# Linear attention into a Swish MLP on one Trainium2 core: a block of small matmuls moved into the output product, and two VectorE differences grouped with a norm multiply

## The chip, the core and the metric

The kernel runs on one core of one Trainium2 chip. The metric is the device time of one execution in microseconds (us): the median of three runs. All other times here are from one profiled execution, counted from the start of its span, whose length is a little under the device time.

The core has five engines, each with its own queue of instructions that it takes in order: TensorE (PE; weight loads are listed apart as PEld), VectorE (DVE), ScalarE (ACT), GpSimd (POOL) and SyncE (SP, which here only issues transfers). They wait for each other through semaphores. TensorE writes only to PSUM, of which there are eight banks (PS0 to PS7 in the kernel).

## The reference, cut to what matters

```
q, k, v: [8 batches, 8 heads, 576, 64]
q_s = softmax(q) over the 64          # exp(q) / sum
k_s = softmax(k) over the 576
kv  = k_s^T v                         # 64 x 64 for each batch and head
x   = q_s kv, heads side by side      # [4608 tokens, 512]
h   = x w_in                          # [4608, 2048]
g   = h * sigmoid(beta * h)
out = g w_out                         # [4608, 512]
```

## The kernel before, in words

**Slabs.** The 4608 tokens are worked in nine slabs. Slab t, for t from 0 to 7, holds the first 512 tokens of batch t; slab 8 holds the remaining 64 tokens of all eight batches. A slab has two passes. Pass 1 makes h and g: 16 tiles of 128 columns of w_in, each from four matmuls (L406) of 128 x 512, then a SiLU on ScalarE (L744) and a scaling by 1/beta on VectorE (L767). Pass 2 makes the output product.

**Pass 2 with seven products.** From slab 1 on, `pass2_fast` uses a scheme of the Strassen kind: in place of eight block products there are seven, each of 16 matmuls of 128 x 256 (L844). The first uses sums of blocks of g (`GS1`), the next two `GS2`, both written during pass 1 (L798, L803); the last two use differences of blocks of g, which `g_diff(0)` and `g_diff(1)` (L810) write in place into GT on VectorE. The combination of the results is on VectorE (TS: L915, L918, L924, L892) and ScalarE (L880). The three accumulators are called s, z5 and z2; z2 is bank OB[1].

**The attention of later batches.** In the same slabs the attention of the next batches is prepared. ScalarE makes exp(q) and exp(k) (L319; for the 64 remaining tokens L331 and L346). `norm_main` makes the softmax of q: VectorE sums (L357) and takes the reciprocal (L359), and the multiply by it (L361) is on GpSimd or on VectorE. `norm_turn` is `norm_main` for two pairs of heads with the multiply on GpSimd, followed by `turn`, a transfer by the DMA engines that transposes EQ into QT (L606). `cast_v` and `cast_vr` convert v on GpSimd (L377, L391). `kv_all` makes k_s^T v with 40 small matmuls (L482), which VectorE scales into KVD (L490, L459). Then `quad` multiplies KVD with QT in 64 x 64 tiles of the TensorE array (L554) and evacuates the results to XT, the input of the next slab's pass 1: blocks 0 and 2 on VectorE, 1 and 3 on ScalarE (L596). From slab 4 on, `quad` also handles the 64 remaining tokens of two batches, from QTR to XT8 (L579).

**What sets the order.** The order within each queue is the order in which the Python code adds instructions. Two devices interleave the work. A counter, `tick`, advances by 1 for each matmul of pass 1 (64 in a slab) and by 32/56 for each matmul of pass 2; a list `todo` names pieces of work with the slot at which they are added, such as slot 97. And `hooks` name work to be added at points of pass 2: `at(0)` ahead of the first product, `at(3)` behind the third, `at(4)` behind the fourth, and so on. So work with a slot over 64 falls into pass 2. Waits are derived from the keys that each instruction reads and writes, and from the PSUM banks that it touches. In `quad` the first matmul takes all the waits of the block: for KVD and QT, and for every bank that it will use, among them those of the last tiles of pass 1.

Three places matter here. In slabs 4 to 6, `quad` for the next batch is added at the head of `pass2_fast`, ahead of `at(0)`, with the line

```
if 3 < t < 7:
    quad(t + 1, (0, 1), t - 3)
```

In slabs 1 and 2, `at(3)` holds `norm_turn(b, 2)` for the second half of the heads, then `g_diff(0)`, then the load of a later batch. In the same slabs `kv_all` is at slot 97, `g_diff(1)` just behind it at 97.01, and the first half of `quad` at 118; its second half follows at slot 1.5 of the next slab. Slab 2 further has, at `at(4)`, exp(q) and the v casts of batch 4. Slab 3 does its `g_diff(1)` and its whole `quad` at slots 99 and 112; slabs 4 to 6 do both differences together behind the third product.

Of the kernel before, what the change touches and what calls it, by code (L numbers as in the profile page):

```python
# [158 lines left out]
def bass_efficient_attn_shen__then__act_swish_beta_kernel(  # L159
# [12 lines left out]
    with ExitStack() as es:  # L172
# [176 lines left out]
        def norm_main(b, hp0, n, eng=DVE, sums=True, mult=True):  # L349
            i = b % 2  # L350
            a = bass.AP(EQ[i], hp0 * 512, [[2048, 128], [64, 8 * n], [1, 64]])
            s_ = bass.AP(QS[i], hp0 * 8, [[32, 128], [1, 8 * n]])
            v_ = bass.AP(QI[i], hp0 * 8, [[32, 128], [1, 8 * n]])
            vb = bass.AP(QI[i], hp0 * 8, [[32, 128], [1, 8 * n], [0, 64]])
            ks = [("eq", i, hp) for hp in range(hp0, hp0 + n)]
            if sums:
                add(DVE, lambda e: e.tensor_reduce(s_, a, AX.X, ALU.add), r=ks,  # L357
                    w=[("qs", i, hp0)])
                add(DVE, lambda e: e.reciprocal(v_, s_), r=[("qs", i, hp0)], w=[("qi", i, hp0)])  # L359
            if mult:  # L360
                add(eng, lambda e: e.tensor_tensor(a, a, vb, ALU.mult), r=ks + [("qi", i, hp0)],  # L361
                    w=ks)
# [35 lines left out]
        def bank(pool=MB):  # L398
            rot[0] += 1
            return pool[rot[0] % len(pool)]  # L400
# [42 lines left out]
        def kd(b):  # L443
            return b if b < 2 else 2 + b % 4
# [89 lines left out]
        def quad(b, gs=(0, 1), pi=None):  # L534
            i = b % 2
            if len(gs) == 1:
                bks = [bank(), bank()]
            else:
                bks = list(MB) + [HB[(hrot[0] + 1) % 3], HB[(hrot[0] + 2) % 3], OB[1]]
            b_x = {2 * g + a: bks[2 * n + a] for n, g in enumerate(gs) for a in range(2)}  # L540
            b_r = bks[4:6]
            rem = pi is not None
            used = list(b_x.values()) + (b_r if rem else [])
            first = [dict(
                r=[k_ for g in gs for c in range(2)
                   for k_ in (("kvd", kd(b), 2 * g + c), ("qt", i, 2 * g + c))]
                + ([("kvd", kd(2 * pi + e_), hp) for e_ in range(2) for hp in range(NHP)]
                   + ["qtr"] if rem else []), bank=used)]

            def tile(o, l, r_, a, c, bk, keys):  # L550
                kw = dict(r=keys, bank=[bk])
                if first:
                    kw = first.pop()
                add(PE, lambda e: e.matmul(o, l, r_, start=True, stop=True,  # L554
                                           tile_position=(64 * a, 64 * c), skip_group_check=True),
                    w=[("ps", bk)], **kw)

            def x_mm(g, a):
                rows = slice(64 * a, 64 * a + 64)
                for c in range(2):  # L560
                    hp, bk = 2 * g + c, b_x[2 * g + a]
                    tile(PS[bk][64 * c:64 * c + 64, :], KVD[kd(b)][rows, hp, 0:D],
                         QT[i][rows, hp, :], a, c, bk, [("kvd", kd(b), hp), ("qt", i, hp)])

            def r_mm(a):
                rows, bk = slice(64 * a, 64 * a + 64), b_r[a]
                for g in range(2):
                    for e_ in range(2):
                        for c in range(2):
                            hp, d, o = 2 * g + c, kd(2 * pi + e_), 128 * g + 64 * e_  # L570
                            tile(PS[bk][64 * c:64 * c + 64, o:o + 64], KVD[d][rows, hp, 0:D],
                                 QTR[rows, hp, 64 * e_:64 * e_ + 64], a, c, bk,
                                 [("kvd", d, hp), "qtr"])

            def r_evac(a):
                bk = b_r[a]
                o = bass.AP(XT8, a * SM + pi * 128, [[NM * SM, 128], [2 * SM, 2], [1, 128]])
                p = bass.AP(PS[bk], 0, [[512, 128], [128, 2], [1, 128]])
                add(DVE, lambda e: e.tensor_copy(o, p), r=[("ps", bk)], w=[("xt8", pi, a)],  # L579
                    bank=[bk])  # L580

            if rem:
                r_mm(1)
                x_mm(0, 0)
                x_mm(0, 1)
                x_mm(1, 0)
                x_mm(1, 1)
                r_mm(0)
                r_evac(1)
            else:  # L590
                for g in gs:
                    for a in range(2):
                        x_mm(g, a)
            for x in sorted(b_x):
                eng, bk = (DVE, ACTE)[x % 2], b_x[x]
                add(eng, lambda e, eng=eng, x=x, bk=bk: (  # L596
                    e.copy if eng == ACTE else e.tensor_copy)(XT[i][:, x, :], PS[bk][:, :]),
                    r=[("ps", bk)], w=[("xt", i, x)], bank=[bk])
            if rem:
                r_evac(0)  # L600

        def turn(b, hp0, n):
            i = b % 2
            o = bass.AP(QT[i], hp0 * 512, [[2048, 128], [128, 4 * n], [1, 128]])
            a = bass.AP(EQ[i], hp0 * 512, [[2048, 128], [1, 512 * n]])
            add(SP, lambda e: e.dma_start_transpose(o, a),  # L606
                r=[("eq", i, hp) for hp in range(hp0, hp0 + n)],
                w=[("qt", i, hp) for hp in range(hp0, hp0 + n)], slot=f"tq{i}{hp0}")
# [14 lines left out]
        def one(fn, *a):  # L623
            return lambda: fn(*a)

        def steps(fn, *a):
            return lambda: go(fn(*a))
# [2 lines left out]
            return kv_steps(b, (0, 1)) + kv_steps(b, (2, 3))  # L630

        def attn(b):
            return [(24 if b == 5 else 16, steps(kv_all, b))]

        def attn_late(b):
            if b < 4:
                return [(97, steps(kv_all, b)), (97.01, lambda: g_diff(1)),
                        (118, one(quad, b, (0,)))]
            return [(96, steps(kv_all, b)), (99, lambda: g_diff(1)), (112, one(quad, b))]

        def spread(steps, lo, hi):
# [9 lines left out]
        def go(steps):  # L651
            for s in steps:
                s()
# [137 lines left out]
        def gv(f, th, n):  # L791
            return GT[:, f:f + n, 256 * th:256 * th + 256]
# [15 lines left out]
        def g_diff(fh):  # L808
            f, th = NG * fh, 1 - fh
            add(DVE, lambda e: e.tensor_tensor(gv(f, th, NG), gv(f, th, NG), gv(f, 1 - th, NG),  # L810
                                               ALU.subtract),
                r=gk(f, 0, NG) + gk(f, 1, NG), w=gk(f, th, NG), war=True)
# [20 lines left out]
        def pass2_fast(t, tick, hooks):  # L833
# [67 lines left out]
                for f in hooks.get(n, ()):  # L901
                    f()

            if 3 < t < 7:
                quad(t + 1, (0, 1), t - 3)
            at(0)
            def prod_s(part):
                prod(s, lambda i, u: GS1[:, i, 128 * u:128 * u + 128], lambda i: [("gs1", i)],
# [46 lines left out]
        for t in range(NSLAB):  # L955
# [88 lines left out]
            def on(n, fn, *a):  # L1044
                hooks.setdefault(n, []).append(lambda: fn(*a))

            def exps(b):
                exp_q(b)
                exp_k(b)
                if b % 2 == 0:  # L1050
                    exp_kr(b)

            def casts(b):
                g = P.writer[("gs2", NG - 1)]
                if b % 2 == 0:
                    cast_vr(b, after=g)
                for hp in range(NHP):
                    cast_v(b, hp, after=g)

            if t == 1:  # L1060
                on(0, exps, 2)
                on(0, casts, 2)
                on(2, norm_turn, 2, 0)
                on(3, norm_turn, 2, 2)
                on(3, g_diff, 0)
                on(3, load, 4)
            elif t == 2:
                on(0, exps, 3)
                on(2, norm_turn, 3, 0)
                on(3, norm_turn, 3, 2)  # L1070
                on(3, g_diff, 0)
                on(3, load, 5)
                on(4, exp_q, 4)
                on(4, casts, 4)
                on(6, norm_turn, 4, 0)
            elif t == 3:
                on(0, exp_k, 4)
                on(0, exp_kr, 4)
                on(0, exp_q, 5)
                on(3, g_diff, 0)  # L1080
                on(4, norm_turn, 5, 0)
                on(5, norm_turn, 5, 2)
                on(4, exp_qr, 1)
                on(5, exp_k, 5)
                on(5, norm_turn_rem)
                on(5, casts, 5)
                on(5, load, 6)
                on(7, load_rem, "qrf", qt_h, QRF, 4)
            elif t + 2 < B:
                b = t + 2  # L1090
                on(0, exps, b)
                on(0, casts, b)
                if t == 4:
                    on(0, load, 7)
                on(3, norm_turn, b, 0)
                on(4, norm_turn, b, 2)
# [40 lines left out]
```

The softmax here doesn't subtract the row's maximum and nothing guards it: scores larger than these inputs give would overflow.

## Time and profile before

| | |
|---|---|
| device time, median of 3 | 275.91 us (275.74 to 276.08) |
| profiled span | 273.8 us |
| TensorE clock granted | 1.00 |
| slab 1, pass 2 | 60.75 to 74.92 |
| slab 2, pass 2 | 89.20 to 103.22 |
| slab 3, pass 2 | 117.66 to 131.41 |
| slabs 4, 5 and 6, from about the end of pass 1 to the end of pass 2 | 146.1 to 160.17, 174.9 to 189.10, 203.6 to 217.85 |
| slab 7, pass 2 (nothing else on TensorE) | 231.90 to 244.13 |

Slab 7 shows what the seven products take alone: 12.23 us. What the other slabs take more is the small matmuls of the attention and the time in which TensorE waits. In the profile's lines, a group is named by the line of the kernel that added it, its engine, operation and operands, with the number of instructions after an x. In the time lines the first number is the start, the second the length, and what stands in brackets at the end is the idle time ahead and what ended it. In the waits the numbers are the total, how often, and the longest.

### The profile page before, as it was taken

To read this page: it belongs to the slowest core of one execution; us is meant where nothing else is said; L and a number is where in the kernel's file an instruction comes from. 1 tells how busy PE (TensorE), PEld (TensorE's weight loads), DVE (VectorE), ACT (ScalarE), POOL (GpSimd) and SP (SyncE) were. 2 spreads that over 40 slices of the span, in tenths; PEclk is the share of its full clock that TensorE was granted. 3 is DMA by queue.
4 is the path that set the end of the run, shared out by engine and by line. 5 is a ranking of instruction groups with operands and counts; after the bars stand their busy time and mean duration, and the time that the engine had idled before them with its cause. 6 is when DMAs were issued, how large, how long until landed. Compare 5 with 4: busy or idle time off the path is not lost.

```text
span 273.8 us, 5005 instructions
## 1 busy us (share of the span) xinstructions
PE 264.2 (97%) x1993; PEld 163.5 (60%) x1993; DVE 192.1 (70%) x407; ACT 181.0 (66%) x287; POOL 62.0 (23%) x80
## 2 busy tenths in 40 slices
PE   8999999999999999999998999899989999999994
PEld 2444444458744874487545864487438845874683
DVE  4964586887868799769778766867586549625762
ACT  4897568788287957797767847793874377008610
POOL 2790010007430099002800470127000100000000
PEclk9999999999999999999999999999999999999999
DMA  7999999989799039920599999203600130012006
GB/s 212 320 204 207 227 329 350 290 246 377 143 347 290 36 73 313 307 78 2 101 342 230 340 319 156 92 4 77 211 2 0 22 153 0 2 47 109 0 0 156
DMA packets 59367, 45.95 MB, mean 168 GB/s; under 512 B 28608, under 2 KB 58320, under 8 KB 58320
## 3 DMA queue, kind: packets, MB, share of 16 engines
q1 hardware_dynamic: 54480, 40.90, 53.4%
q0 software_dynamic: 4240, 4.19, 9.3%
q10 hardware_dynamic: 624, 0.53, 0.6%
q8 instruction: 16, 0.26, 0.4%
q14 instruction: 7, 0.06, 0.1%
HBM read 36.71 MB, written 9.44 MB: 169 GB/s over the span
## 4 chain that ended last, share of the span: by engine, by line
PE 82%; DVE 7%; DMA 4%; POOL 2%; SPq 2%; issue 1%; ACT 1%; POOLq 0%; DVEq 0%
PE PS L406 49%; PE PS L844 30%; DMA VF<-in_v_dram 2%; DVE QS L357 2%; PE PS L554 1%; DMA QT<-EQ 1%; ACT GT L744 1%; DVE GT L810 1%; PE PS L482 1%; POOL VB L377 1%; SPq L290 1%; SPq L278 1%; DVE EQ L361 1%; POOL EQ L361 1%; DVE VB L377 1%
## 5 line engine op out<-in xcount | busy, mean ns | idle before, releaser
L406 PE MATMUL PS<-XT,WIN 128*128 128x512 bf16 x576 | 127.9, 379 | 0.1
L744 ACT ACTIVATE GT<-PS,BETA 128x512 bf16<-128x512 f32 x144 | 95.0, 689 | 37.2 <-PE PS L406 36.9
L406 PEld LDWEIGHTS PS<-XT,WIN 128*128 128x128 bf16 x576 | 54.9, 98 | 65.0 <-DVE XT L596 0.8
L767 DVE TENSOR_SCALAR GT<-GT,RB 128x512 bf16<-128x512 bf16 x144 | 52.6, 386 | 38.9 <-ACT GT L744 38.1
L361 POOL TENSOR_TENSOR EQ<-EQ,QI 128x1024 bf16<-128x1024 bf16 (+1 forms) x13 | 25.6, 1967 | 50.3 <-DVE QI L359 49.6
L844 PE MATMUL PS<-WOUT,GS 128*128 128x256 bf16 x256 | 30.6, 273 | 0.0
L844 PE MATMUL PS<-WSUM,GT 128*128 128x256 bf16 x256 | 29.9, 273 | 0.3 <-DVE GT L810 0.3
L844 PE MATMUL PS<-WOUT,GT 128*128 128x256 bf16 x256 | 29.8, 273 | 0.0
L880 ACT COPY O2S<-PS 128x512 f32<-128x512 f32 (+1 forms) x17 | 9.4, 559 | 28.4 <-PE PS L844 28.3
L844 PEld LDWEIGHTS PS<-WSUM,GT 128*128 128x128 bf16 x256 | 24.8, 98 | 4.1 <-issue 1.3
L844 PEld LDWEIGHTS PS<-WOUT,GS 128*128 128x128 bf16 x256 | 25.1, 98 | 2.9
L844 PEld LDWEIGHTS PS<-WOUT,GT 128*128 128x128 bf16 x256 | 24.8, 98 | 3.0
L319 ACT ACTIVATE EQ<-QF 128x512 bf16<-128x512 f32 x32 | 17.9, 619 | 7.7 <-DMA QF<-in_q_dram 7.5
L803 DVE TENSOR_TENSOR GS<-GT 128x512 bf16<-128x512 bf16 (+2 forms) x32 | 21.9, 685 | 0.0
L810 DVE TENSOR_TENSOR GT<-GT 128x2048 bf16<-128x2048 bf16 x16 | 21.2, 1353 | 0.0
L357 DVE TENSOR_REDUCE QS<-EQ 128x16 f32<-128x1024 bf16 (+1 forms) x20 | 19.7, 984 | 0.8 <-ACT EQ L319 0.8
L377 POOL CAST VB<-VF 128x512 bf16<-128x512 f32 x24 | 14.7, 613 | 22.7 <-DVE GS L803 13.8
L319 ACT ACTIVATE EK<-KF 128x512 bf16<-128x512 f32 x32 | 18.1, 620 | 0.2 <-DMA KF<-in_k_dram 0.2
L892 DVE TENSOR_TENSOR O2S<-TS,PS 128x512 f32<-128x512 f32 (+1 forms) x17 | 10.7, 644 | 9.3 <-PE PS L844 9.3
L844 PE MATMUL PS<-WSUM,GS 128*128 128x256 bf16 x128 | 16.6, 273 | 0.0
L406 PE MATMUL PS<-WOUT,GT 128*128 128x512 bf16 x64 | 15.4, 379 | 0.0
L798 DVE TENSOR_TENSOR GS<-GT 128x256 bf16<-128x256 bf16 (+2 forms) x32 | 13.6, 426 | 1.1
(88 smaller groups left out, 206.8 us busy)
## 6 DMA issues: line engine op xcount, KB each, us to landing
out_dram<-O2S SPq DMA_DIRECT2D x8, 1024.0 KB, 5.0
QF<-in_q_dram SPq DMA_DIRECT2D x6, 1024.0 KB, 6.6
KF<-in_k_dram SPq DMA_DIRECT2D x6, 1024.0 KB, 9.3
VF<-in_v_dram SPq DMA_DIRECT2D x6, 1024.0 KB, 12.4
KF<-in_k_dram SPq DMA_DIRECT2D x8, 256.0 KB, 5.6
VF<-in_v_dram SPq DMA_DIRECT2D x8, 256.0 KB, 5.6
WOUT<-in_moe_w_out_dram POOLq DMA_DIRECT2D x4, 512.0 KB, 16.5
WIN<-in_moe_w_in_dram POOLq DMA_DIRECT2D x3, 512.0 KB, 9.2
```

The lines of the kernel that those rows point to most:

```text
L319: add(ACTE, lambda e, o=o, a=a: e.activation(o, a, ACT.Exp), r=[(name + "f", i, hp)], w=[("e" + name, i, hp)])
L357: add(DVE, lambda e: e.tensor_reduce(s_, a, AX.X, ALU.add), r=ks, w=[("qs", i, hp0)])
L361: add(eng, lambda e: e.tensor_tensor(a, a, vb, ALU.mult), r=ks + [("qi", i, hp0)], w=ks)
L377: add(eng, lambda e: (e.copy if eng == ACTE else e.tensor_copy)(o, a), r=[("vf", i, hp), ("vone", i)], w=[("vb", i, hp)], after=after)
L406: add(PE, lambda e: e.matmul(o, l, r_, start=start, stop=stop), r=r, w=w, bank=[bk])
L744: add(ACTE, lambda e: e.activation(GT[:, f, :], PS[bk][:, :], ACT.Silu, scale=BETA[:, f:f + 1]), r=[("ps", bk), "beta"], w=[("gt", f, 0), ...
L767: add(DVE, lambda e: e.tensor_scalar(GT[:, f, :], GT[:, f, :], RB[:, f:f + 1], None, ALU.mult), r=k + ["rb"], w=k)
L798: add(DVE, lambda e: e.tensor_tensor(GS1[:, i:i + n, :], gv(i, 0, n), gv(i + NG, 1, n), ALU.add), r=gk(i, 0, n) + gk(i + NG, 1, n), w=[("g ...
L803: add(DVE, lambda e: e.tensor_tensor(GS2[:, i:i + n, :], GT[:, i:i + n, :], GT[:, i + NG:i + NG + n, :], ALU.add), r=[k_ for f in (i, i + ...
L810: add(DVE, lambda e: e.tensor_tensor(gv(f, th, NG), gv(f, th, NG), gv(f, 1 - th, NG), ALU.subtract), r=gk(f, 0, NG) + gk(f, 1, NG), w=gk(f ...
L844: add(PE, lambda e, l=l, r_=r_, st=st, u=u, i=i, b_=b_: e.matmul(PS[b_][:, 256 * u:256 * u + 256], l, r_, start=st, stop=end and i == NG - ...
L892: add(DVE, lambda e, b_=b_, u0=u0, u1=u1: e.tensor_tensor(o[:, u0:u1, :], ts[:, u0:u1, :], bank3(b_)[:, u0:u1, :], ALU.add), r=["ts", ("ps ...
```

## The change

It has two parts. In slabs 4 to 6 the block of 64 x 64 matmuls is no longer added ahead of the output product but at slot 72 of the `todo` list, so eight slots, or 14 matmuls of pass 2, after pass 1 ends. Its purpose is to let TensorE start the product while the last tile of pass 1 is still being read from PSUM.

In slabs 1 and 2, both differences stand together at `at(3)`, and the second multiply of the norm is taken from GpSimd to VectorE and put behind them: sums and reciprocal, two differences, multiply, transposing transfer. `g_diff(1)` leaves slot 97.01, and slab 1's `kv_all` moves from slot 97 to 100. Its purpose is to keep GpSimd's multiply out of the way of the differences.

```diff
         def attn(b):
-            return [(24 if b == 5 else 16, steps(kv_all, b))]
+            return [(24 if b == 5 else 16, steps(kv_all, b)),
+                    (72, one(quad, b, (0, 1), b - 4))]
 
         def attn_late(b):
             if b < 4:
-                return [(97, steps(kv_all, b)), (97.01, lambda: g_diff(1)),
-                        (118, one(quad, b, (0,)))]
+                return [(100 if b == 2 else 97, steps(kv_all, b)), (118, one(quad, b, (0,)))]
...
-            if 3 < t < 7:
-                quad(t + 1, (0, 1), t - 3)
             at(0)
...
+            def diffs_norm(b):
+                norm_main(b, 2, 2, mult=False)
+                g_diff(0)
+                g_diff(1)
+                norm_main(b, 2, 2, sums=False)
+                turn(b, 2, 2)
+
...
-                on(3, norm_turn, 2, 2)
-                on(3, g_diff, 0)
+                on(3, diffs_norm, 2)
...
-                on(3, norm_turn, 3, 2)
-                on(3, g_diff, 0)
+                on(3, diffs_norm, 3)
```

## The prediction

> **What bounds the kernel now.** I read the page's busy shares first, then the chain of waits, then TensorE's waits, then the time lines of the slabs that the diff touches. All times are microseconds from the span's start.
>
> ```profile
> PE 264.2 (97%) x1993; PEld 163.5 (60%) x1993; DVE 192.1 (70%) x407; ACT 181.0 (66%) x287; POOL 62.0 (23%) x80
> ```
>
> TensorE is busy for 97%. Only what stops TensorE, or adds to its list, changes the time; the other engines count where TensorE waits for them. The chain that ended last shows the stops of slab 4, and the same at 175.05 and 203.81 for slabs 5 and 6:
>
> ```profile
> 137.51 8.75 PE PS L406 x40
> 146.29 0.70 ACT GT L744
> 146.98 0.25 issue
> 147.23 0.77 PE PS L554 x20
> 148.00 12.33 PE PS L844 x112
> ```
>
> Columns: start, length, what. The chain leaves TensorE for the SiLU of the last tile of pass 1 (ACT GT L744), crosses a 0.25 hand-over and comes back with the small matmuls of `quad` (L554). In TensorE's waits it is the largest entry:
>
> ```profile
> PE PS L554 <- ACT GT L744: 2.9, 3, 1.0
> ```
>
> Three waits, 2.9 together. The product (L844) behind them needs none of this. Slab 2, by engine: VectorE and GpSimd.
>
> ```profile
> 97.23 1.26 DVE L810 TENSOR_TENSOR GT<-GT 128x2048 bf16<-128x2048 bf16 x1
> 98.41 0.16 DVE L490 RECIPROCAL RC<-PS 128x2 f32<-128x2 f32 x1
> 98.60 0.29 DVE L459 TENSOR_TENSOR KVD<-PS,RC 128x128 bf16<-128x128 f32 x1
> 98.81 0.16 DVE L490 RECIPROCAL RC<-PS 128x2 f32<-128x2 f32 x1
> 99.00 0.29 DVE L459 TENSOR_TENSOR KVD<-PS,RC 128x128 bf16<-128x128 f32 x1
> 99.20 2.12 DVE L810 TENSOR_TENSOR GT<-GT 128x2048 bf16<-128x2048 bf16 x1
> ```
> ```profile
> 95.50 4.74 POOL L361 TENSOR_TENSOR EQ<-EQ,QI 128x1024 bf16<-128x1024 bf16 x2 [13.77 <-DVE QI L359]
> 100.38 2.16 POOL L391 CAST VR<-VRF 64x512 bf16<-64x512 f32 x2
> 102.67 2.64 POOL L377 CAST VB<-VF 128x512 bf16<-128x512 f32 x4
> ```
>
> The reader should see two differences of one size at 1.26 and 2.12, and two GpSimd multiplies at 4.74 where one alone takes 1.90: they took turns. And TensorE in slabs 1 and 2:
>
> ```profile
> 67.80 0.22 PE L482 MATMUL PS<-VR,EKR 128*64 128x65 bf16 x2 [0.30 <-ACT EKR L331]
> ...
> 72.71 0.41 PE L554 MATMUL PS<-QT,KVD 64*64 64x512 bf16 x4
> ```
> ```profile
> 100.58 0.41 PE L554 MATMUL PS<-QT,KVD 64*64 64x512 bf16 x4
> 100.92 0.28 PE L844 MATMUL PS<-WSUM,GT 128*128 128x256 bf16 x1
> 101.47 1.91 PE L844 MATMUL PS<-WSUM,GT 128*128 128x256 bf16 x16 [0.27 <-DVE GT L810]
> ```
>
> The 40 small matmuls of `kv_all` (L482) stop for exp(k) of the remainder in slab 1; in slab 2 the last product stops for the second difference. The last entry of each line is the idle time and what ended it. For prices, the groups by shape:
>
> ```profile
> L361 DVE TENSOR_TENSOR EQ<-EQ,QI 128x512 bf16<-128x512 bf16 x7 | 5.1, 723 | 0.2
> ```
>
> [...] the second multiply (start 97.48, 2.76) is longer by 0.86 beside the first difference, and the second difference by 0.86 beside that multiply. [...] The norm multiply has a float32 factor; its median at 512 elements is 691 ns[...]. [...] In slab 3, where `quad` already stands inside a product, its start came 0.19 after the last full matmul's start instead of the usual 0.11: 0.08 for the switch in.
>
> **Part 1: the quads of slabs 4 to 6 move from the head of pass 2 to slot 72.** Pass 1 has 64 slots, a matmul of pass 2 counts 32/56, so slot 72 is 14 matmuls in. The last pass-1 matmul of slab 4 starts at 145.87; at that pace (0.216) the next could start at 146.09, and `quad` starts at 147.23: a stop of 1.14. Afterwards the first 14 product matmuls go there. They need bank `s`, whose SiLU ended at 145.25, and sums GS1 0 to 5 and GS2 0, done before 146. They last 14 x 0.109 = 1.53, so `quad` comes at 147.6, after the SiLU has been seen (147.23): no wait. It adds the switch in, 0.08 to 0.12. Saved: 1.14 - 0.10 = 1.04 per slab, 3.1 for three.
>
> What moves with it: on ScalarE the casts of x=1 and x=3 fall behind the exponentials. From table load to exp(q) remainder that is 155.52 - 148.92 = 6.6; from 146.98 it ends at 153.6, the two casts (1.07) at 154.7, and the copy of z5 (0.58) at 155.2. TensorE wants that bank at 156.68 - 1.04 = 155.6: hidden, by 0.4 less hand-over. The next readers of XT come with the next slab. On VectorE the four evacuations last from 147.94 to 149.88 today; moved, they are released by 148.0 and end near 149.9, and the TS copy queued behind them wants to start at 151.20 - 1.04 = 150.16: hidden. So is the product that needs the bank OB[1], at 150.3.
>
> **Part 2, slab 1.** Removed: a GpSimd multiply (1.90), which overlaps, and the stop for exp(k) of the remainder, since `kv_all` starts 3 slots = 5 matmuls = 0.55 later (67.73, the operand is there at 67.74, wanted 0.15 into the block). `kv_all` took 1.24 (67.18 to 68.42) and 0.76 in slab 2: 0.48 saved there. Added on VectorE: from 68.78 two differences at 1.18 start to start (2.35 for two where nothing interferes), to 71.14, then the multiply, [...] next instruction after 1.14: 72.28. No GpSimd work is queued in this stretch. Behind it stand RC and KVD (0.49); TensorE waits for KVD with `quad` of heads 0,1: 72.28 + 0.49 + 0.15 hand-over = 72.92, against 72.71. It would have arrived near 72.1, so the 0.48 goes into this wait and 0.2 is lost. The transpose of the second half is issued at 72.36 instead of 71.82 and lands 3.1 later, at 75.5; the second `quad` half is wanted at 75.65: hidden. With 3.7, as the first transpose took, it would cost 0.4. Slab 1: +0.2.
>
> **Part 2, slab 2.** Here GpSimd is not idle: with its second multiply gone, the casts for batch 4 follow at once (ready, since they start without a wait today). The first VR cast is waiting when the first difference ends at 98.41, so I let the two engines alternate as in the lines above: cast (0.55, the end of the stretched one: 101.25 to 101.80), second difference, cast, multiply. 98.41 + 0.5 + 1.1 + 0.5 + 1.1 = 101.6, with slab 1's 0.2, 101.8; KVD and hand-over 0.64: `quad` at 102.4 against 100.58, +1.8. From there to the first pass-1 matmul that needs the third XT block, VectorE has the block, a sum, a reduction with reciprocal, a sum and the next block, 3.8 plus 0.6, against 4.55 today (100.58 to 105.13): -0.15. The second difference is no longer waited for, which is inside that 4.55. Slabs 1 and 2 together: **+1.65**. Nothing gives it back: TensorE runs pass 1 of slab 3 without gaps.
>
> Sum: 275.91 - 3.1 + 1.65 = **274.5**.
>
> **The rivals.** (a) [...] For it: they are queued back to back, and no GpSimd instruction in this trace waits at the seam of two such instructions, so that the seam's winner isn't shown. Against: at 134.49 and 135.09, between casts started at 133.74, 134.41 and 135.08, VectorE's scalings took 0.6 instead of 0.35: the engines alternate. Then the multiply ends at 97.23 + 2.36 + 1.14 + 0.2 = 100.9, `quad` starts at 101.6, slabs 1 and 2 cost 0.85: 273.7. (b) Half of part 1 is lost, to a dearer switch of array modes in mid-product or to ScalarE's later casts and copy: -1.5, and the slabs' +1.65: 276.1, no change. For it: the margin of 0.4 on ScalarE in slab 4. Against: slab 5 has no remainder of k (0.5 less on ScalarE) and slab 6 no exponentials but one; slab 3's `quad` in mid-product shows no such cost. (c) Slower: the same with the slow transpose (+0.4) and one more GpSimd cast of 0.6 ahead of the multiply: 277.1. Against it: the casts have to come in just at each gap.
>
> **How the numbers follow.** Alternation 0.58, (a) 0.26, (b) 0.09, (c) 0.07. Faster is the first two, 0.84. The range goes from (a) with 0.4 more (the switches free, 0.3, and slab 1 nearer to no loss, 0.1), 273.3, to the forecast with 1.0 more (transpose 0.4, one more cast 0.6), 275.5; beyond lie (b) and (c).
>
> **What would show it.** Right: no TensorE wait of L554 on ACT GT L744 and some 27.7 instead of 28.75 (slab 6: 189.10 to 217.85) per slab for 4 to 6; in slab 1 no wait on EKR but `quad` held by KVD; in slab 2 VectorE's second difference and multiply lengthened by about 0.5 beside VR casts, and `quad` near 102.4. Wrong: `quad` in slab 2 before 101.8 (then (a)), or a new wait of L844 on ACT O2S or DVE in slabs 4 to 6 (then (b)).

## The result, and the profile after

| | before | changed | ratio (95% interval) |
|---|---|---|---|
| device time, median of 6 | 275.89 us | 274.42 us (274.0 to 274.77) | 0.9947 (0.9934 to 0.996) |
| profiled span | 273.8 us | 272.4 us | |

The changed kernel is faster by 1.5 us, against a forecast of 1.4. The two parts work against each other: the first gives about three microseconds, the second takes more than half of them back.

TensorE's waits in the changed kernel (total, how often, longest):

```profile
PE PS L554 <- DVE RC L490: 1.5, 1, 1.5
...
PE PS L554 <- DVE KVD L459: 1.0, 1, 1.0
```

The entry of L554 on ACT GT L744, 2.9 us in three waits, is gone. In its place stand two waits of the same small matmuls, one in each of slabs 1 and 2. The profile puts both down to VectorE; in slab 1 the transposed QT landed later than KVD was written, as shown below. The chain that ended last, at the seam of slab 4:

```profile
139.35 8.58 PE PS L406 x39
147.93 1.64 PE PS L844 x15
149.57 0.70 PE PS L554 x20
150.27 10.69 PE PS L844 x97
```

The chain no longer leaves TensorE here: pass 1, 1.64 us of product, `quad`, the rest of the product. It is 15 matmuls of the product that go ahead, not the 14 named above: 14 steps of 32/56 add up in floating point to just under 8, so slot 72 is reached at the fifteenth. The first pass-1 matmuls of slabs 4 to 7 now start at 133.31, 161.02, 188.72 and 216.43: 27.7 us a slab. Before it was 131.41, 160.17, 188.93 and 217.69: 28.76 a slab. (The table ahead ends slabs 5 and 6 with the last product matmul, 0.17 later.)

Now slab 2, where the time is lost. VectorE, then GpSimd, then TensorE in time lines of the changed kernel:

```profile
97.57 2.80 DVE L810 TENSOR_TENSOR GT<-GT 128x2048 bf16<-128x2048 bf16 x2
100.29 1.63 DVE L361 TENSOR_TENSOR EQ<-EQ,QI 128x1024 bf16<-128x1024 bf16 x1
101.85 0.16 DVE L490 RECIPROCAL RC<-PS 128x2 f32<-128x2 f32 x1
102.04 0.29 DVE L459 TENSOR_TENSOR KVD<-PS,RC 128x128 bf16<-128x128 f32 x1
```
```profile
95.84 1.90 POOL L361 TENSOR_TENSOR EQ<-EQ,QI 128x1024 bf16<-128x1024 bf16 x1 [13.77 <-DVE QI L359]
97.88 2.97 POOL L391 CAST VR<-VRF 64x512 bf16<-64x512 f32 x2
```
```profile
99.13 1.80 PE L844 MATMUL PS<-WSUM,GT 128*128 128x256 bf16 x15
102.47 0.41 PE L554 MATMUL PS<-QT,KVD 64*64 64x512 bf16 x4 [1.55 <-DVE RC L490]
...
106.82 1.47 PE L406 MATMUL PS<-XT,WIN 128*128 128x512 bf16 x6 [0.23 <-DVE XT L596]
```

Two VR casts that take 1.35 us when alone (in the run with held casts, below) now take 2.97, and the VectorE instructions beside them are longer too. KVD, which used to be written at 98.6, is written at 102.04 and ends at 102.33; 0.14 later `quad` starts. The profile names RC L490 as the releaser, which is the second reciprocal, started at 102.25; by the keys `quad` waits for the KVD ahead of it.

Slab 1 has no GpSimd work at that place, and its lines are the undisturbed price:

```profile
68.72 2.39 DVE L810 TENSOR_TENSOR GT<-GT 128x2048 bf16<-128x2048 bf16 x2
71.04 1.21 DVE L361 TENSOR_TENSOR EQ<-EQ,QI 128x1024 bf16<-128x1024 bf16 x1
72.17 0.16 DVE L490 RECIPROCAL RC<-PS 128x2 f32<-128x2 f32 x1
72.36 0.29 DVE L459 TENSOR_TENSOR KVD<-PS,RC 128x128 bf16<-128x128 f32 x1
```

2.39 against 2.80 and 1.21 against 1.63: each of the two casts adds 0.41 to 0.42 us in slab 2.

What `quad` waits for in slab 1 is the later of two: the KVD that its first half reads ended at 72.65, but the transpose of the first half of the heads took 4.1 us to land, until 73.0. `quad` started just behind it:

```profile
L606 SPq DMA_TRANSPOSE QT<-EQ x1: 1347/1347/1347, 68.9 to 68.9; - x1
...
DMA to landing us min/median/max: 4.1/4.1/4.1
```
```profile
73.05 0.41 PE L554 MATMUL PS<-QT,KVD 64*64 64x512 bf16 x4 [0.97 <-DVE KVD L459]
```

### The profile page after: what moved, and what is told of

It reads as the page before. It is cut to its first block, busy times and chain, and to the rows that moved or that the text cites. A ratio compares the mean times of both kernels' runs of the same rounds, so it can differ in the third digit from the quotient of the medians.

```text
span 272.4 us, 4985 instructions
## 1 busy us (share of the span) xinstructions
PE 262.3 (96%) x1974; PEld 163.5 (60%) x1993; DVE 193.9 (71%) x409; ACT 180.8 (66%) x287; POOL 58.8 (22%) x78
## 4 chain that ended last, share of the span: by engine, by line
PE 81%; DVE 12%; DMA 2%; SPq 2%; issue 1%; ACT 0%; DVEq 0%
PE PS L406 48%; PE PS L844 30%; DVE QS L357 3%; DMA VF<-in_v_dram 2%; DVE GT L810 2%; DVE EQ L361 2%; PE PS L554 1%; PE PS L482 1%; SPq L278 1%; SPq L290 1%; DVE QI L359 1%; DVE O2S L892 1%; DVE VB L377 1%; DVE TS L913 1%; DVE TS L916 1%
## 5 line engine op out<-in xcount | busy, mean ns | idle before, releaser
L406 PE MATMUL PS<-XT,WIN 128*128 128x512 bf16 x560 | 125.4, 379 | 1.5 <-issue 0.3
L744 ACT ACTIVATE GT<-PS,BETA 128x512 bf16<-128x512 f32 x144 | 95.0, 689 | 37.4 <-PE PS L406 37.2
L844 PE MATMUL PS<-WOUT,GS 128*128 128x256 bf16 x256 | 31.1, 273 | 0.0
L361 POOL TENSOR_TENSOR EQ<-EQ,QI 128x1024 bf16<-128x1024 bf16 (+1 forms) x11 | 20.0, 1822 | 50.5 <-DVE QI L359 50.2
L844 PE MATMUL PS<-WOUT,GT 128*128 128x256 bf16 x256 | 29.8, 273 | 0.0
L844 PE MATMUL PS<-WSUM,GT 128*128 128x256 bf16 x256 | 29.8, 273 | 0.0
L880 ACT COPY O2S<-PS 128x512 f32<-128x512 f32 (+1 forms) x17 | 9.4, 560 | 27.6 <-PE PS L844 27.6
L844 PEld LDWEIGHTS PS<-WSUM,GT 128*128 128x128 bf16 x256 | 24.8, 98 | 3.7 <-issue 0.9
L844 PEld LDWEIGHTS PS<-WOUT,GT 128*128 128x128 bf16 x256 | 24.8, 98 | 2.9
L844 PEld LDWEIGHTS PS<-WOUT,GS 128*128 128x128 bf16 x256 | 24.8, 98 | 3.0
L377 POOL CAST VB<-VF 128x512 bf16<-128x512 f32 x24 | 16.4, 682 | 25.4 <-DVE GS L803 13.2
L810 DVE TENSOR_TENSOR GT<-GT 128x2048 bf16<-128x2048 bf16 x16 | 20.3, 1301 | 0.0
L844 PE MATMUL PS<-WSUM,GS 128*128 128x256 bf16 x128 | 16.6, 273 | 0.0
L844 PEld LDWEIGHTS PS<-WSUM,GS 128*128 128x128 bf16 x128 | 12.5, 98 | 3.2
```

The lines of the kernel that those rows point to most:

```text
L377: add(eng, lambda e: (e.copy if eng == ACTE else e.tensor_copy)(o, a), r=[("vf", i, hp), ("vone", i)], w=[("vb", i, hp)], after=after)
L406: add(PE, lambda e: e.matmul(o, l, r_, start=start, stop=stop), r=r, w=w, bank=[bk])
L744: add(ACTE, lambda e: e.activation(GT[:, f, :], PS[bk][:, :], ACT.Silu, scale=BETA[:, f:f + 1]), r=[("ps", bk), "beta"], w=[("gt", f, 0), ...
L844: add(PE, lambda e, l=l, r_=r_, st=st, u=u, i=i, b_=b_: e.matmul(PS[b_][:, 256 * u:256 * u + 256], l, r_, start=st, stop=end and i == NG - ...
L880: add(eng, lambda e, b_=b_, u0=u0, u1=u1: (e.copy if eng == ACTE else e.tensor_copy)(o[:, u0:u1, :], bank3(b_)[:, u0:u1, :]), r=[("ps", b_ ...
```

## The experiments

All times are medians with the ratio to the kernel before on the same chip (275.7 us there).

**Part 1 alone.** The diff's lines for slabs 4 to 6 only.

> Part 1 alone: quad of slabs 4 to 6 at slot 72, slabs 1 and 2 as before. My theory: each of the three slabs loses the stop of 1.14 us and pays about 0.1 for the switch of array tiling, so -3.1 us: 272.8 us, and 27.7 us a slab as in the changed kernel. Rival: part 1 brings only the 1.5 us that the whole change brought, and part 2 costs nothing: 274.4 us.

Measured: 273.02 us, ratio 0.9899 (0.9886 to 0.9913). In its trace the slabs start at 131.05, 158.75, 186.46 and 214.16: 27.7 us each, 1.06 less than before, so 3.2 us by the trace and 2.8 us (2.4 to 3.1) by the ratio. The rival, that part 1 gives only what the whole gave, is out.

**Part 2 alone.** The diff's lines for slabs 1 and 2 only.

> Part 2 alone: differences and VectorE multiply together in slabs 1 and 2, quad of slabs 4 to 6 at the head of pass 2 as before. My theory: slower by 1.65 us, 277.5 us, with quad of slab 1 near 73.0 and of slab 2 near 102.4, both held by KVD on VectorE. Rival: taking GpSimd's multiply out of the differences' way is a gain, 275.9 us or less.

Measured: 277.37 us, ratio 1.0062 (1.0048 to 1.0076): slower by 1.7 us. `quad` came at 72.89 and 102.31. KVD of the first heads ended at 72.74 and the transposed half had landed by 72.4 in slab 1, so there KVD ended last. Part 2 as a whole is a loss. The two parts add up within their intervals: -1.0% and +0.6% against -0.5% together.

**Part 1, shorter way in.** Part 1 with slot 67 for `quad`, so 6 product matmuls go ahead of it and not 15.

```diff
-                    (72, one(quad, b, (0, 1), b - 4))]
+                    (67, one(quad, b, (0, 1), b - 4))]
```

> Part 1 alone with quad at slot 67 in place of 72: 6 product matmuls (0.65 us) go ahead of it and not 14. My theory (what is hidden is the wait for the last tile's SiLU): 0.65 of the 1.14 us is filled, some 0.45 us of wait for ACT GT L744 stays in each of slabs 4 to 6, the switch hides in it: -1.95 us, 273.95 us. Rival (the gain comes from the place of quad or from the order on ScalarE, whatever the distance): the same as slot 72, 272.8 us.

Measured: 273.54 us, ratio 0.9916 (0.9904 to 0.9928). TensorE in slab 4:

```profile
145.88 0.82 PE L845 MATMUL PS<-WSUM,GS 128*128 128x256 bf16 x6
146.92 0.22 PE L554 MATMUL PS<-QTR,KVD 64*64 64x64 bf16 x3 [0.21 <-ACT GT L745]
```

A part of the wait stays, and the slabs are 28.0 us long, between 28.76 and 27.7. The 0.21 is idle time behind the end of the last matmul, which was 0.98 before. Counted as in the expectation, from where the next matmul could have started, it is 0.38 against the expected 0.45. The last SiLU ended 0.89 us behind that point in the traces of the kernel before and of the changed one, which here puts its end, by estimate, at 146.77 and the hand-over at 0.15 us in place of 0.25. So the gain follows the amount of product put ahead of `quad`. It is the slabs of the trace that show it: the interval of the ratio overlaps that of slot 72.

**ScalarE's order alone.** `quad` stays ahead of the product, but is added behind the hooks of `at(0)`.

```diff
-            if 3 < t < 7:
-                quad(t + 1, (0, 1), t - 3)
             at(0)
+            if 3 < t < 7:
+                quad(t + 1, (0, 1), t - 3)
```

> The kernel before, with quad of slabs 4 to 6 still ahead of the product but added behind the hooks of at(0): on ScalarE the exponentials then stand ahead of the XT casts, as in the change, and TensorE's order is untouched. My theory: no change, 275.9 us, the wait for ACT GT L744 stays at 2.9 us. Rival (the gain is from ScalarE starting its table load and exponentials 1.9 us earlier): -3 us or a good part of it.

Measured: 275.61 us, ratio 0.9992 (0.9984 to 1.0001). ScalarE's table load starts at 146.69, at once behind the last SiLU, and TensorE waits as it did:

```profile
146.92 0.22 PE L554 MATMUL PS<-QTR,KVD 64*64 64x64 bf16 x3 [0.98 <-ACT GT L744]
```

ScalarE's earlier start alone is worth nothing that this measurement can tell; the gain is TensorE's order.

**GpSimd's casts held back in slab 2.** The changed kernel, and the v casts of batch 4 also wait for the multiply.

```diff
-                g = P.writer[("gs2", NG - 1)]
+                g = P.writer[("gs2", NG - 1)] + (P.writer[("eq", 1, 2)] if b == 4 else [])
```

> The changed kernel, but slab 2's v casts of batch 4 on GpSimd also wait for VectorE's multiply. My theory: the second difference and the multiply of slab 2 are stretched by two VR casts (0.45 and 0.4 us by the trace: 2.80 against 2.39 for the pair, 1.63 against 1.21), so quad of slab 2 comes 0.9 us earlier, near 101.6, and the time is 273.5 us. Rival: the stretch has another cause or is made up elsewhere: 274.4 us.

Measured: 273.32 us, ratio 0.9912 (0.9898 to 0.9926); the interval lies below that of the changed kernel. VectorE and GpSimd in slab 2:

```profile
97.16 2.39 DVE L810 TENSOR_TENSOR GT<-GT 128x2048 bf16<-128x2048 bf16 x2
99.48 1.21 DVE L361 TENSOR_TENSOR EQ<-EQ,QI 128x1024 bf16<-128x1024 bf16 x1
```
```profile
100.85 1.35 POOL L391 CAST VR<-VRF 64x512 bf16<-64x512 f32 x2 [3.51 <-DVE RC L490]
```

Both VectorE lengths fall back to those of slab 1, the casts to 1.35, `quad` comes at 101.24. So the stretch comes with the overlap of the two engines' work: 0.41 and 0.42 us on VectorE, 1.62 on GpSimd. Not all of the 1.1 us between the two medians hangs on it. From the start of slab 2's product to that of slab 3's it is 28.98 us here, 29.81 in the changed kernel and 28.46 before. So of the 1.35 us that slab 2 had lost, the casts are 0.83; the other 0.52 is the new order on VectorE. Slab 1, which this edit leaves alone, is 0.25 us shorter than in the changed kernel's trace: there the first transpose landed after 3.1 us and not 4.1.

**The multiply back on GpSimd.** The changed kernel with both differences together, but:

```diff
-                norm_main(b, 2, 2, mult=False)
+                norm_main(b, 2, 2, POOL)
+                turn(b, 2, 2)
                 g_diff(0)
                 g_diff(1)
-                norm_main(b, 2, 2, sums=False)
-                turn(b, 2, 2)
```

> The changed kernel, but the multiply of slabs 1 and 2 is back on GpSimd; both differences stay together at at(3). My theory: [...] the second difference ends near 72.9 in slab 1 and KVD behind it near 73.4, so quad comes 0.5 us later there (73.5) and some 0.3 us later in slab 2: 274.8 us. Rival: the multiply on VectorE is the cost of part 2, and without it quad comes 1.1 us earlier in each slab: 273 us or less.

Measured: 274.60 us, ratio 0.9957 (0.9945 to 0.9969), like the changed kernel. Slab 1:

```profile
68.84 4.10 DVE L810 TENSOR_TENSOR GT<-GT 128x2048 bf16<-128x2048 bf16 x2
72.86 0.15 DVE L490 RECIPROCAL RC<-PS 128x2 f32<-128x2 f32 x1
```

Two differences take 4.10 in place of 2.39: GpSimd's multiply gets in between. `quad` comes at 73.49, and at 102.65 in slab 2. Taking the multiply out of VectorE's queue gains nothing: in slab 1 it stretches the differences ahead of KVD by 1.7 us, where on VectorE it took 1.1 to the next instruction. In slab 2, where the casts now come behind it, KVD starts 4.2 us behind the first difference, against 4.5 in the changed kernel.

**KVD first.** The changed kernel; at `at(3)` only the sums and `g_diff(0)` stay, and `g_diff(1)`, the multiply and the transpose go behind `kv_all`.

```diff
-                g_diff(1)
-                norm_main(b, 2, 2, sums=False)
-                turn(b, 2, 2)
...
+                        (100.01 if b == 2 else 97.01, one(diff_norm, b)),
```

> The changed kernel, but in slabs 1 and 2 only the sums and the first difference stay at at(3); the second difference, the multiply and the transpose follow kv_all's KVD on VectorE. My theory: quad's first half no longer waits for KVD (slab 1 near 72.7, slab 2 near 100.6), but the transposes are issued later (about 73.1 and 102.3), so quad's second half waits for QT: near 76.2 in slab 1 (75.8 in the changed kernel) and 105.6 in slab 2 (105.2): 274.6 us, no gain, the wait only changes its place. Rival: the order ahead of KVD is all of the cost, so most of 1.65 us comes back: 273.0 us.

Measured: 296.35 us, ratio 1.0757 (1.0728 to 1.0786). A miss by 22 us, and explained by neither theory. SyncE's queue in slab 1:

```profile
69.01 1.34 SPq L606 DMA_TRANSPOSE QT<-EQ  x1
70.40 0.57 SPq L278 DMA_DIRECT2D QF<-in_q_dram  x1
71.03 1.05 SPq L278 DMA_DIRECT2D KF<-in_k_dram  x1
72.12 1.10 SPq L278 DMA_DIRECT2D VF<-in_v_dram  x1
73.26 4.64 SPq L285 DMA_DIRECT2D KRF<-in_k_dram  x2
77.94 4.24 SPq L285 DMA_DIRECT2D VRF<-in_v_dram  x2
82.23 2.67 SPq L606 DMA_TRANSPOSE QT<-EQ  x1
```

The loads of a later batch are added at `at(3)`, and by moving the transpose behind them I had turned the order of the two in SyncE's queue. The multiply ended at 73.1, the transpose was issued at 82.23, and `quad`'s second half started at 86.94 after 10.96 us of idle TensorE. Three waits for QT add up to 20.3 us. The mean granted clock of the six runs was 0.956 to 0.964, against 0.997 to 1.0 in those of the kernel before on the same chip, and TensorE was slower behind the two longest waits: 61 matmuls of pass 1 took 15.93 and 15.19 us there, against 13.57 in the run that follows, which adds to the loss. That run put the loads back behind the transpose, with this edit on top:

```diff
-                on(3, load, 4)
-                on(3, load, 5)
...
             turn(b, 2, 2)
+            load(b + 2)
```

> As kv_first, but the loads of the later batch (for slabs 1 and 2) are added behind the second transpose, as in the kernel before, and not ahead of it. My theory for the 20 us of kv_first: there the transpose stood behind 3.25 MB of loads in SyncE's queue and on the DMA engines, and was issued at 82.2 although the multiply ended at 73.1. With the loads behind it, the first expectation of kv_first should hold: quad's first half no longer held by KVD, its second half held by QT, about 274.6 us (273.8 to 275.4). Rival: the order on VectorE (second difference and multiply behind KVD) is itself the cause, and the time stays near 296 us; or, no wait takes its place, 273.0 us.

Measured: 276.77 us (275.39 to 278.51 over 22 runs, a wider spread than the other kernels'), ratio 1.004 (1.0026 to 1.0054). The 20 us were the order in SyncE's queue (the loads ahead of the transpose were 3.5 MB, not the 3.25 of the expectation). The time is above the range I gave. The nine runs above 277 us had a mean granted clock of 0.992 to 0.994, the five below 276 us one of 0.999 to 1.0; the profile is of a run of 276.08 us and doesn't show that part. TensorE in it:

```profile
72.76 0.41 PE L554 MATMUL PS<-QT,KVD 64*64 64x512 bf16 x4 [0.81 <-DMA QT<-EQ]
...
77.07 0.41 PE L554 MATMUL PS<-QT,KVD 64*64 64x512 bf16 x4 [1.51 <-DMA QT<-EQ]
...
107.16 0.41 PE L554 MATMUL PS<-QT,KVD 64*64 64x512 bf16 x4 [1.95 <-DMA QT<-EQ]
```

KVD no longer holds anything (it ended at 70.25 in slab 1), and the wait is now for the transposed QT. It is larger than I had worked out: the multiply ended at 72.9 in slab 1, but its transpose took 4.1 to land instead of 3.1; in slab 2 the casts stretched the second difference (1.56) and the multiply (1.62) again. Why the landings differ was not tried.

**Part 1 with slab 1's later `kv_all`.** In `attn_late`, on top of part 1:

```diff
-                return [(97, steps(kv_all, b)), (97.01, lambda: g_diff(1)),
+                x = 100 if b == 2 else 97
+                return [(x, steps(kv_all, b)), (x + 0.01, lambda: g_diff(1)),
```

> Part 1, and of part 2 only slab 1's kv_all at slot 100 (g_diff(1) still directly behind it). The stop of kv_all for exp(k) of the remainder (0.48 us in slab 1) goes. My theory: quad of slab 1 then waits for the transposed QT, which landed at 72.65 while quad started at 72.71, so at most 0.1 us comes of it: 272.7 us. Rival: all of the 0.48 is gained: 272.3 us.

Measured: 272.81 us, ratio 0.9898 (0.9884 to 0.9912): the same as part 1 alone. My size was right, its reason only in part. `quad`'s first half did come earlier (71.88 against 72.35 with part 1 alone), just behind QT, which landed at 71.8; then the last product stopped for the second difference:

```profile
72.73 1.91 PE L846 MATMUL PS<-WSUM,GT 128*128 128x256 bf16 x16 [0.23 <-DVE GT L812]
```

The second half of `quad` came at 75.00 against 75.08. The wait taken away came back behind it.

## Why the prediction was right

By its own steps:

- *Part 1, a stop of 1.14 filled, 0.10 paid for the switch, 3.1 us for three slabs.* The slabs are 1.06 us shorter each in the trace of the changed kernel and of part 1 alone, 3.2 us; the ratio of part 1 alone gives 2.8 us (2.4 to 3.1). That the filled wait is the SiLU's is shown by slot 67. That ScalarE's later casts are hidden is shown by the changed kernel's waits, where none of L844 on O2S L880 stands. The 14 matmuls were 15, which changes nothing: both counts are longer than the wait. The switch was 0.09: in each of the three slabs `quad` starts 0.20 us behind the start of the last product matmul ahead of it, where product matmuls follow each other in 0.11; in slab 3 of the kernel before it is the same 0.20, not 0.19.
- *Slab 1, +0.2.* From the start of slab 1's product to that of slab 2's it is 28.85 us in the changed kernel's trace (60.69 to 89.54) against 28.45 before (60.75 to 89.20): +0.40, twice the forecast. The stop for exp(k) is gone, and its gain went into the wait ahead of `quad`, both as forecast. What came on top is the first transpose: the forecast named KVD as the last to end, and there it was QT, landed at 73.0. It had reckoned with a late landing, but of the second transpose. In the trace of part 2 alone it was KVD, as forecast, and slab 1 lost 0.15. The 1.14 from the start of the multiply to the next instruction was an estimate, as the kernel before has no multiply of 1024 elements on VectorE. Its trace leads to the same figure: 0.29 us at 128 elements (L459) and 0.69 at 512 (L361) make about 1.23 at 1024, less the 0.08 by which the next instruction started before the end of the first difference (1.26 and 1.18). Measured: 1.21 long, 1.13 to the next.
- *Slab 2, casts in turn with VectorE.* `quad` was forecast at 102.4 and came at 102.47, and the run with held casts shows the cause. The likeliest rival, (a), in which no cast gets in between VectorE's three instructions, fell here: the casts came in at both seams, with 0.41 and 0.42 us. The third XT block then sets the pace, as forecast: the first matmul that needs it, at 106.82 and after a stop of 0.23, is 4.35 us behind `quad`, forecast 4.4. Slab 2 lost 1.35 us in both traces, forecast 1.45.
- *The second difference that TensorE waited for before*: its wait is gone in the changed kernel, as forecast.

Slabs 1 and 2 together, forecast at 1.65 us, lost 1.75 in the changed kernel's trace and 1.50 in that of part 2 alone, whose ratio gives 1.7. The mechanism is the forecast's. That the total came out so close is in part luck: in the changed kernel's trace slab 1 lost 0.2 more than forecast, slab 2 and part 1 were each 0.1 better.

For the order with KVD first I had worked out VectorE and TensorE and left out who else stands in SyncE's queue.

The fastest medians are those of part 1 without the rest: 273.0 us, or 272.8 us with slab 1's later `kv_all`, which the measurement doesn't tell apart; nor does it tell them from slot 67 (273.5) or from the changed kernel with held casts (273.3), whose intervals overlap theirs. So no run shows a gain from the new order of slabs 1 and 2, and as it stands in the changed kernel it is a loss. In the old order VectorE writes KVD between the two differences, while GpSimd multiplies.

## What to carry to other kernels

When a block of matmuls waits for the last PSUM reader of the stage before, put as much independent TensorE work ahead of it as the wait is long. Here 0.65 us of product shortened the slab by 0.76 us (about 0.1 of it, by the estimate above, a shorter hand-over), and 1.64 us by 1.06, which is about the wait of 1.14 less the switch of 0.09; a longer stretch was not tried. Before an instruction is moved to a busy queue, ask what stands behind it there and which engine waits for that: here a multiply that nobody waited for on GpSimd went ahead of a scaling that TensorE waits for. And an engine relieved of work starts its next work earlier; ask what that collides with.

## What the runs showed of the hardware

- In slab 2 of the changed kernel two 64 x 512 casts on GpSimd, each begun 0.95 us before a difference on VectorE ended, got in at both seams, between the two differences and between the second and the multiply: 0.41 and 0.42 us on the VectorE side, 2.97 us in place of 1.35 on theirs. With the multiply back on GpSimd, 1.90 us where it is alone, two differences took 4.10 us against 2.39.
- A transpose of 128 x 1024 elements, issued with no load just ahead of it, landed 3.1 to 4.1 us after its issue in slabs 1 and 2. Two that follow in slab 3 behind a batch's loads took 8.0 and 7.5 us in the kernel before, 9.2 and 6.9 in the changed one.
- With KVD first, a transpose placed behind the loads of a batch (three of 1 MB and four of 128 KB) was issued 9.1 us after the multiply that it needs had ended (73.1 and 82.23).
